# Masked softmax of an attention stage: exponent and mask read the scaled scores from the PSUM score banks, or from a float32 copy in SBUF

## Chip, cores and metric

The kernel runs on one core of a Trainium2 chip. The metric is the device time of one execution in microseconds (us), lower is better. In the profile PE is TensorE (matmuls), PEld its weight loads, DVE is VectorE, ACT is ScalarE, POOL is GpSimd and SP is SyncE. PSUM is the memory that TensorE writes its results to (8 banks of 512 float32 per partition); SBUF is the larger on-chip memory. TensorE writes to PSUM only, and GpSimd does not read PSUM in this program.

## What is computed

Three stages follow each other. The change lies in the first, the attention, with q, k and v of shape (4, 8, 576, 64), so 32 heads:

```python
scale = 1.0 / np.sqrt(q.shape[-1])
scores = scale * np.matmul(q, k.transpose(0, 1, 3, 2))
thresh = np.max(scores, axis=-1, keepdims=True) - tau
scores = np.where(scores >= thresh, scores, -1000000000.0)
scores = scores - np.max(scores, axis=-1, keepdims=True)
attn = np.exp(scores)
attn = attn / (np.sum(attn, axis=-1, keepdims=True) + 1e-09)
return np.matmul(attn, v).astype(np.float32)
```

Its output (2304 tokens of 512) goes through a gated layer, `(x @ w_a) * (x @ w_b) @ w_out`, and then through a second layer with a softmax-like activation and a layer norm. Everything is float32; the two later stages split each operand into a high and a low part and use three matmuls for each product.

## The kernel before

**Work of the attention stage.** Two heads make a pair; there are NP = 16 pairs. A pair has NS = 9 units of 128 score rows (two heads times four blocks of 128 queries, and one unit that holds the last 64 queries of both heads), each 576 keys wide, which makes 144 units. The loop over `m` takes two units a step, called A and B here, so 72 steps work on new scores and nine steps make two pairs.

**What a unit passes through.** `scores` (line 277) multiplies q and k into one of two PSUM buffers `ps`, each of two banks. `soft_max` (line 283, DVE) reads the scores, multiplies them by -SCALE, takes the row minimum of the products into `nm`, and writes the products to a bfloat16 tile `junk` that nobody reads and of which there is one buffer. `soft_exp` (line 295, ACT) reads the scores from `ps` again and writes exp(SCALE * score + nm) to `pe` (`pet` for the unit of the last queries). `soft_thr` (line 300, POOL) turns `nm` into the threshold `th`, a column of 128 numbers. `soft_mask` (line 309, DVE) reads the scores from `ps` a third time, compares them with `th`, multiplies `pe` by the comparison in place, and sums each row into `z`. Below, these four are called max, exp, threshold and mask. One step later the masked unit is transposed on TensorE (`tpose`, line 329, into `tp`; `tpose_tail`, lines 345 and 348, into `tq`), copied to SBUF by ACT (line 322), and some steps later multiplied with v (`pv`, line 360, into `po`; copied out by ACT at line 368). Line 381 transposes the reciprocals of the row sums.

**What sets the order.** The order is written out by hand and kept by a manual schedule: each engine works through its own instructions in the order in which the program issues them. Within a step it is the string

```python
PROG = 'ABtVFTUYaufbz'
```

`A` and `B` are scores, max and exp of the two units, `t` and `u` the two thresholds, `a` and `b` the two masks; `V` are the products with v, `F` the transposed reciprocals, `T`, `U` and `Y` the transposes of the units of the step before. `f` and `z` are filling work on DVE: the reciprocal of the row sums (lines 315 and 316) or one of three operations (lines 125, 128 and 131) that assemble later stages' weights from pairs of 32-bit words. At the end of a step ACT gets the copies (lines 322, 368) and parts of the same weight conversion (lines 121 and 135), POOL the last part of it (line 138), and SP the loads. So DVE's order in a step is max A, max B, mask A, filling work, mask B, filling work, and TensorE's is scores A, scores B, products with v, transposes.

**Who waits for whom.** The waits are put in from the buffers: scores A of a step take the `ps` buffer of unit A of the step before, and must wait until its last reader is done with it; the same holds for B.

Of the kernel before, what the change touches and what calls it, by code (L numbers as in the profile page):

```python
# [8 lines left out]
F32 = mybir.dt.float32  # L9
F32R = mybir.dt.float32r  # L10
BF16 = mybir.dt.bfloat16
U32 = mybir.dt.uint32
U64 = mybir.dt.uint64
AF = mybir.ActivationFunctionType
ALU = mybir.AluOpType
AX = mybir.AxisListType
PSUM = bass.MemoryType.PSUM
P = 128
# [3 lines left out]
def kernel(  # L22
# [11 lines left out]
    nc = tc.nc  # L34
    NP, _, VS, D = v.shape
# [11 lines left out]
    HS = S // 2  # L47
# [9 lines left out]
    SCALE = 1.0 / float(D) ** 0.5  # L57
    BIG = 3.0e38
# [13 lines left out]
    taub = const.tile([P, 1], F32, name="taub")  # L72
    neg = const.tile([P, 1], F32, name="neg")
    toff = const.tile([P, 1], F32, name="toff")
# [144 lines left out]

    def tau_consts():  # L220
        nc.vector.tensor_scalar(out=neg, in0=taub, scalar1=0.0, scalar2=None, op0=ALU.is_lt)
        nc.vector.tensor_scalar(out=taub, in0=taub, scalar1=-1.0 / SCALE, scalar2=None, op0=ALU.mult)
        nc.vector.scalar_tensor_tensor(out=toff, in0=neg, scalar=BIG, in1=taub, op0=ALU.mult, op1=ALU.add)

    def attention():
        es = ExitStack()
# [2 lines left out]
        pp = es.enter_context(tc.tile_pool(name="pp", bufs=3))  # L229
# [5 lines left out]
        st = {}  # L235
# [42 lines left out]
            st[i, s] = ps  # L278

        def soft_max(i, s, nm):  # L280
            ps = st[i, s]
            junk = pp.tile([P, 2, HS], BF16, name="junk", bufs=1)
            nc.vector.tensor_scalar(out=junk, in0=ps[:, :, 0:HS], scalar1=-SCALE, scalar2=None, op0=ALU.mult, op1=ALU.min, accum_out=nm)  # L283
            st[i, s] = (ps, nm)

        def soft_exp(i, s):
            ps, nm = st[i, s]
            if s < 2 * NQ:
                qc, h = divmod(s, 2)
                if h == 0:  # L290
                    st[i, "p", qc] = pp.tile([P, 2, S], F32, name="pe", bufs=4)
                pe = st[i, "p", qc][:, h]
            else:
                pe = pp.tile([P, S], F32, name="pet", bufs=2)
            nc.scalar.activation(out=pe.rearrange("p (g s) -> p g s", g=2), in_=ps[:, :, 0:HS], func=AF.Exp, bias=nm, scale=SCALE)  # L295
            st[i, s] = [ps, pe, nm]

        def soft_thr(nm):
            th = sm.tile([P, 1], F32, name="th")
            nc.gpsimd.tensor_scalar(out=th, in0=nm, scalar1=-1.0 / SCALE, scalar2=toff, op0=ALU.mult, op1=ALU.add)  # L300
            return th

        def soft_mask(i, s, th):
            ps, pe, _ = st[i, s]
            if s == 0:
                st[i, "z"] = sm.tile([P, NS], F32, name="z", bufs=2)
            z = st[i, "z"]
            pv = pe.rearrange("p (g s) -> p g s", g=2)
            nc.vector.scalar_tensor_tensor(out=pv, in0=ps[:, :, 0:HS], scalar=th, in1=pv, op0=ALU.is_ge, op1=ALU.mult, accum_out=z[:, s:s + 1])  # L309
            st[i, s] = pe  # L310

        def recip(i):
# [82 lines left out]
        for h in range(2):  # L395
# [4 lines left out]
            if h == 0:  # L400
                nc.scalar.dma_start(out=taub, in_=tau.to_broadcast([P, 1]))
        tau_consts()
        alloc_qk(1)
        load_k(1)
# [15 lines left out]
        for m in range(tot // 2 + 6):  # L420
# [9 lines left out]
            nm = {}  # L430
            th = {}

            def score(k):
                if k < len(cur):
                    nm[k] = sm.tile([P, 1], F32, name="nm")
                    scores(*cur[k])
                    soft_max(*cur[k], nm[k])
                    soft_exp(*cur[k])

            def thr(k):  # L440
                if k < len(cur):
                    th[k] = soft_thr(nm[k])

            def mask(k):
                if k < len(cur):
                    soft_mask(*cur[k], th[k])
                    if cur[k][1] == NS - 1:
                        recip(cur[k][0])
# [32 lines left out]
            i, s = divmod(2 * m, NS)  # L481
# [312 lines left out]
```

## Time and profile before

| what | us |
|---|---|
| median of three runs (992.99, 994.72, 995.31) | 994.72 |
| the profiled execution: its own time | 994.94 |
| the profiled execution: span from first to last instruction | 993.2 |
| attention stage: first max to the last mask's end | 7.4 to 302.5 |
| PE, DVE, ACT, POOL busy, whole span | 958.6, 552.1, 461.8, 196.1 |

A row of the timeline reads: start in us from the span's start, duration in us, engine, line of the kernel, operation, out<-in by the program's names, and in brackets how long the engine had been idle before and who ended that. Several instructions of one kind in a row are merged (x2, x8), and then the duration is that of all of them. A max or a mask is followed by a short DVE_READ_ACCUMULATOR that writes out its row result. In a group the columns are operation, names, shapes, count | busy us, mean ns of one | idle time before it and its cause. The granted TensorE clock is 0.997 of full speed over the span.

### The profile page before, as it was taken

The page shows a single profiled execution, that of the slowest core. Times are in us where ns is not written, and L with a number is a line of the kernel's source. Part 1 is how long each engine was busy: PE and PEld are TensorE (multiplying, and loading weights), DVE is VectorE, ACT ScalarE, POOL GpSimd, SP SyncE. Part 2 cuts the span into 40 slices and gives each one's busy share as a digit, 9 for nine tenths or more (in the row PEclk, how much of TensorE's full clock was granted, in tenths as well). Part 3 has the DMA queues.
Part 4 walks back from the last instruction along what each step waited for, and adds up shares of the span by engine and source line. Part 5 has one row for each costly group of instructions (what it writes and reads, how often), then busy time and mean ns, then how long its engine had stood idle before and what let it go on. Part 6 is the DMA issues. An engine that isn't in the chain of part 4 may idle for free.

```text
span 993.2 us, 17033 instructions
## 1 busy us (share of the span) xinstructions
PE 958.6 (97%) x6464; PEld 797.9 (80%) x6464; DVE 552.1 (56%) x1262; ACT 461.8 (47%) x889; POOL 196.1 (20%) x294
## 2 busy tenths in 40 slices
PE   6999898999899999999999999999999999999997
PEld 3555555555558999999999999999999788888885
DVE  5888888877887665553222666322322544444443
ACT  4777777777775444443222444211221434333332
POOL 1111112111113311220000333000001233333331
PEclk9999999999999999999999999999999999999999
DMA  5423532432615655444210554222102111111100
GB/s 140 143 85 96 157 103 84 132 96 82 165 59 176 204 169 155 142 134 122 92 49 24 179 156 154 72 73 72 47 26 94 32 50 47 46 49 45 44 22 32
DMA packets 56002, 95.59 MB, mean 96 GB/s; under 512 B 15088, under 2 KB 33648, under 8 KB 55920
## 3 DMA queue, kind: packets, MB, share of 16 engines
q1 hardware_dynamic: 55488, 93.91, 31.0%
q8 instruction: 51, 0.84, 0.4%
q10 hardware_dynamic: 432, 0.59, 0.2%
q14 instruction: 31, 0.25, 0.1%
HBM read 70.80 MB, written 23.68 MB: 95 GB/s over the span
## 4 chain that ended last, share of the span: by engine, by line
PE 83%; DVE 10%; issue 2%; ACT 2%; DMA 1%; POOL 1%; SPq 0%; DVEq 0%; ACTq 0%
PE ps L542 29%; PE py L564 15%; PE po L698 10%; PE ps L646 9%; PE ps L277 7%; PE po L360 7%; PE tp L329 5%; DVE junk L283 3%; DVE pe L309 2%; PE pl L679 1%; DVE pet L309 1%; PE tq L345 1%; DMA wraw<-in_w_dram 1%; DMA k<-in_qkv_dram 1%; DVE w L131 0%
## 5 line engine op out<-in xcount | busy, mean ns | idle before, releaser
L542 PE MATMUL ps<-xt,w 128*128 128x288 f32 x2304 | 321.4, 295 | 0.3 <-DVE g L549 0.2
L542 PEld LDWEIGHTS ps<-xt,w 128*128 128x128 f32 x2304 | 310.9, 188 | 0.7 <-DVE g L549 0.7
L564 PE MATMUL py<-gt,w 128*128 128x288 f32 x1152 | 168.1, 295 | 0.0
L564 PEld LDWEIGHTS py<-gt,w 128*128 128x128 f32 x1152 | 158.0, 188 | 0.0
L549 DVE TENSOR_TENSOR g<-ps,a 128x288 f32<-128x288 f32 x96 | 43.8, 457 | 192.7 <-ACT a L548 192.7
L138 POOL TENSOR_TENSOR w<-w,w 128x512 fp32r<-128x512 f32 x52 | 77.9, 1498 | 289.9 <-ACT w L135 289.9
L283 DVE TENSOR_SCALAR_CACHE_REDUCE junk<-ps 128x576 bf16<-128x576 f32 x144 | 109.0, 757 | 43.2 <-PE ps L277 34.5
L277 PE MATMUL ps<-k,q 64*128 64x288 f32 (+1 forms) x640 | 105.8, 450 | 25.7 <-DVE pe L309 15.8
L548 ACT ACTIVATE a<-ps 128x288 f32<-128x288 f32 x96 | 39.3, 409 | 187.3 <-PE ps L542 187.3
L295 ACT ACTIVATE pe<-ps,nm 128x576 f32<-128x576 f32 x128 | 94.8, 743 | 66.3 <-DVE junk L283 65.3
L698 PE MATMUL po<-w,lt 128*128 128x512 f32 x432 | 104.5, 395 | 2.6 <-ACT lt L684 1.3
L309 DVE SCALAR_TENSOR_TENSOR pe<-ps,th,pe 128x576 f32<-128x576 f32 x128 | 104.0, 816 | 5.0 <-POOL th L300 3.2
L646 PE MATMUL ps<-w,ys 128*128 128x512 f32 x432 | 105.2, 398 | 1.3 <-POOL ys L518 1.3
L698 PEld LDWEIGHTS po<-w,lt 128*128 128x128 f32 x432 | 80.4, 187 | 23.6 <-ACT lt L684 2.2
L277 PEld LDWEIGHTS ps<-k,q 64*128 64x128 f32 (+1 forms) x640 | 47.3, 179 | 62.3 <-issue 26.4
L646 PEld LDWEIGHTS ps<-w,ys 128*128 128x128 f32 x432 | 79.6, 187 | 20.3 <-POOL ys L518 1.7
L322 ACT ACTIVATE pt<-tp 128x512 f32<-128x512 f32 (+1 forms) x160 | 79.0, 552 | 7.7 <-PE tp L329 5.8
L300 POOL TENSOR_SCALAR th<-nm,toff 128x1 f32<-128x1 f32 x144 | 38.1, 265 | 216.3 <-DVE junk L283 214.2
L360 PE MATMUL po<-pt,vr 128*64 128x322 f32 (+1 forms) x512 | 78.3, 427 | 0.1
L329 PEld LDWEIGHTS tp<-ident,pe 128*128 128x128 f32 x512 | 58.0, 145 | 24.8 <-issue 17.4
L329 PE MATMUL tp<-ident,pe 128*128 128x128 f32 x512 | 72.9, 285 | 0.9 <-ACT pt L322 0.9
L551 DVE TENSOR_TENSOR gt<-g,gt 128x288 fp32r<-128x288 f32 x96 | 44.0, 458 | 49.1 <-ACT gt L550 49.1
(73 smaller groups left out, 802.3 us busy)
## 6 DMA issues: line engine op xcount, KB each, us to landing
wraw<-in_w_dram SPq DMA_DIRECT2D x36, 512.0 KB
q<-in_qkv_dram SPq DMA_DIRECT2D x15, 576.0 KB
k<-in_qkv_dram SPq DMA_DIRECT2D x30, 176.0 KB
xd<-xp SPq DMA_DIRECT2D x16, 289.0 KB
xr<-xd SPq DMA_DIRECT2D x8, 576.0 KB
zr<-rzd SPq DMA_DIRECT2D x16, 288.0 KB
xsd<-xr SPq DMA_DIRECT2D x8, 576.0 KB
ypd<-y SPq DMA_DIRECT2D x8, 576.0 KB
```

Source lines behind the costliest of these rows:

```text
L138: nc.gpsimd.tensor_tensor(out=w["o"][1], in0=w["f"] if wide else raw, in1=w["o"][0].bitcast(F32), op=ALU.subtract)
L277: nc.tensor.matmul(ps[rows, g, 0:HS], lhsT=q[r, u, c], rhs=k[r, u, o:o + HS], start=True, stop=True, skip_group_check=True)
L283: nc.vector.tensor_scalar(out=junk, in0=ps[:, :, 0:HS], scalar1=-SCALE, scalar2=None, op0=ALU.mult, op1=ALU.min, accum_out=nm)
L295: nc.scalar.activation(out=pe.rearrange("p (g s) -> p g s", g=2), in_=ps[:, :, 0:HS], func=AF.Exp, bias=nm, scale=SCALE)
L309: nc.vector.scalar_tensor_tensor(out=pv, in0=ps[:, :, 0:HS], scalar=th, in1=pv, op0=ALU.is_ge, op1=ALU.mult, accum_out=z[:, s:s + 1])
L322: evac_q.append(lambda: nc.scalar.activation(out=out, in_=in_, func=AF.Copy))
L329: nc.tensor.transpose(tp[:, kc, :], pe[:, o:o + P], ident)
L360: nc.tensor.matmul(po[h * D:(h + 1) * D], lhsT=lhsT, rhs=rhs, start=(kc == 0), stop=(kc == NQ), skip_group_check=True)
L542: nc.tensor.matmul(pa[:, 0:NB], lhsT=wt[:, m, wi, kc * P:(kc + 1) * P], rhs=xt[:, kc, xi, :], start=(k == 0), stop=(k == 3 * KC - 1))
L564: nc.tensor.matmul(py, lhsT=wt[:, 2, wi, oc * P:(oc + 1) * P], rhs=gt[:, gi, :], start=(first and k == 0), stop=(last and k == 2))
L646: nc.tensor.matmul(ph[:, g, :], lhsT=y[:, a, kc, :], rhs=w2(2 * kc + g, b), start=(k == 0), stop=(k == 3 * KC - 1))
L698: nc.tensor.matmul(po, lhsT=lt[:, a, j, :], rhs=w2(2 * KC + j, b), start=(k == 0), stop=(k == 3 * NJ - 1))
```

## The change

The max now writes its products, -SCALE times the scores, as float32 to a new SBUF tile `ns` with four buffers, in place of the bfloat16 `junk`. The exp reads `ns` with scale -1, and the mask reads `ns` and compares with "less or equal", so that neither touches `ps` any more. The threshold is formed in the scaled domain; one tiny instruction of the preparation goes.

```diff
     def tau_consts():
         nc.vector.tensor_scalar(out=neg, in0=taub, scalar1=0.0, scalar2=None, op0=ALU.is_lt)
-        nc.vector.tensor_scalar(out=taub, in0=taub, scalar1=-1.0 / SCALE, scalar2=None, op0=ALU.mult)
-        nc.vector.scalar_tensor_tensor(out=toff, in0=neg, scalar=BIG, in1=taub, op0=ALU.mult, op1=ALU.add)
+        nc.vector.scalar_tensor_tensor(out=toff, in0=neg, scalar=-BIG, in1=taub, op0=ALU.mult, op1=ALU.add)
...
         def soft_max(i, s, nm):
-            ps = st[i, s]
-            junk = pp.tile([P, 2, HS], BF16, name="junk", bufs=1)
-            nc.vector.tensor_scalar(out=junk, in0=ps[:, :, 0:HS], scalar1=-SCALE, scalar2=None, op0=ALU.mult, op1=ALU.min, accum_out=nm)
-            st[i, s] = (ps, nm)
+            ns = pp.tile([P, 2, HS], F32, name="ns", bufs=4)
+            nc.vector.tensor_scalar(out=ns, in0=st[i, s][:, :, 0:HS], scalar1=-SCALE, scalar2=None, op0=ALU.mult, op1=ALU.min, accum_out=nm)
+            st[i, s] = (ns, nm)
...
-            nc.scalar.activation(out=pe.rearrange("p (g s) -> p g s", g=2), in_=ps[:, :, 0:HS], func=AF.Exp, bias=nm, scale=SCALE)
-            st[i, s] = [ps, pe, nm]
+            nc.scalar.activation(out=pe.rearrange("p (g s) -> p g s", g=2), in_=ns, func=AF.Exp, bias=nm, scale=-1.0)
+            st[i, s] = (ns, pe)
...
-            nc.gpsimd.tensor_scalar(out=th, in0=nm, scalar1=-1.0 / SCALE, scalar2=toff, op0=ALU.mult, op1=ALU.add)
+            nc.gpsimd.tensor_scalar(out=th, in0=nm, scalar1=1.0, scalar2=toff, op0=ALU.mult, op1=ALU.add)
...
-            nc.vector.scalar_tensor_tensor(out=pv, in0=ps[:, :, 0:HS], scalar=th, in1=pv, op0=ALU.is_ge, op1=ALU.mult, accum_out=z[:, s:s + 1])
+            nc.vector.scalar_tensor_tensor(out=pv, in0=ns, scalar=th, in1=pv, op0=ALU.is_le, op1=ALU.mult, accum_out=z[:, s:s + 1])
```

No instruction changes its place on its engine; what differs are the operands, and with them the waits that stand in front of instructions. Lines after the first of these edits move up: in the changed kernel scores are line 276, max 281, exp 293, threshold 298, mask 307, transposes 327.

On DVE, two steps around a weight conversion, first before. The brackets give the engines whose progress the instruction waits for (`DVE_49` is DVE's own, `PE_49` TensorE's).

```order
L283 TENSOR_SCALAR junk,nm<-ps 128x576 [waits DVE_49,PE_49] x2
L309 SCALAR_TENSOR_TENSOR pe,z<-ps,th,pe 128x576 [waits Activation_49,Pool_49]
L125 TENSOR_SCALAR wlow<-wraw 128x512 [waits DMAHW3_49]
L309 SCALAR_TENSOR_TENSOR pe,z<-ps,th,pe 128x576 [waits Activation_49,Pool_49]
L128 SCALAR_TENSOR_TENSOR wlow<-wraw,wlow 128x512 [waits DVE_49]
L283 TENSOR_SCALAR junk,nm<-ps 128x576 [waits PE_49]
L283 TENSOR_SCALAR junk,nm<-ps 128x576 [waits DVE_49,PE_49]
```

The same place in the changed kernel:

```order
L281 TENSOR_SCALAR ns,nm<-ps 128x576 [waits PE_49] x2
L307 SCALAR_TENSOR_TENSOR pe,z<-ns,th,pe 128x576 [waits Activation_49,Pool_49]
L125 TENSOR_SCALAR wlow<-wraw 128x512 [waits DMAHW3_49]
L307 SCALAR_TENSOR_TENSOR pe,z<-ns,th,pe 128x576 [waits Activation_49,Pool_49]
L128 SCALAR_TENSOR_TENSOR wlow<-wraw,wlow 128x512 [waits DVE_49]
L281 TENSOR_SCALAR ns,nm<-ps 128x576 [waits PE_49] x2
```

The order is the same; max B no longer waits for an earlier instruction of DVE (the one buffer of `junk` is gone).

On TensorE, the transposes of one step and the scores of the next, before:

```order
L329 MATMUL tp<-ident,pe 128x128 [waits Activation_49]
L329 MATMUL tp<-ident,pe 128x128 x3
L277 MATMUL ps<-k,q 128x288 [waits DVE_49,PE_49]
L277 MATMUL ps<-k,q 128x288
```

and in the changed kernel:

```order
L327 MATMUL tp<-ident,pe 128x128 [waits DVE_49,Activation_49]
L327 MATMUL tp<-ident,pe 128x128 x3
L276 MATMUL ps<-k,q 128x288 [waits DVE_49]
L276 MATMUL ps<-k,q 128x288
```

Both versions let the scores wait for DVE, but for another instruction: the last reader of `ps` was the mask and is now the max. The transposes now carry a wait for DVE of their own, for the mask whose output they read; before, the scores ahead of them in TensorE's order had waited for that mask already.

## Rows read from the trace of the kernel before

**Rows 1.** Windows: busy us of each engine in nine steps of the attention stage.

```profile
103.19:139.99 36.80, 33.98 (x252) 19.78 (x250) 31.14 (x83) 27.70 (x52) 7.32 (x20) 1.00 0.36 112
```

**Rows 2.** Waits from 5 to 303 us: in total us, times, longest us.

```profile
DVE junk L283 <- PE ps L277: 34.5, 50, 2.4
...
PE ps L277 <- DVE pe L309: 15.8, 20, 1.7
```

**Rows 3.** Timeline: a step without filling work (DVE, ACT and POOL).

```profile
132.05 0.75 DVE L283 TENSOR_SCALAR_CACHE_REDUCE junk<-ps 128x576 bf16<-128x576 f32 x1
...
132.84 0.74 ACT L295 ACTIVATE pet<-ps,nm 128x576 f32<-128x576 f32 x1 [0.92 <-DVE junk L283]
132.93 0.76 DVE L283 TENSOR_SCALAR_CACHE_REDUCE junk<-ps 128x576 bf16<-128x576 f32 x1
...
133.68 0.82 DVE L309 SCALAR_TENSOR_TENSOR pet<-ps,th,pet 128x576 f32<-128x576 f32 x1
133.73 0.74 ACT L295 ACTIVATE pe<-ps,nm 128x576 f32<-128x576 f32 x1 [0.15 <-DVE junk L283]
133.87 0.26 POOL L300 TENSOR_SCALAR th<-nm,toff 128x1 f32<-128x1 f32 x1 [0.63 <-DVE junk L283]
...
134.57 0.82 DVE L309 SCALAR_TENSOR_TENSOR pe<-ps,th,pe 128x576 f32<-128x576 f32 x1
...
135.45 0.76 DVE L283 TENSOR_SCALAR_CACHE_REDUCE junk<-ps 128x576 bf16<-128x576 f32 x1
```

**Rows 4.** Timeline of DVE: mask A, L125, mask B, L128, next max.

```profile
113.31 0.82 DVE L309 SCALAR_TENSOR_TENSOR pe<-ps,th,pe 128x576 f32<-128x576 f32 x1
...
114.39 0.81 DVE L309 SCALAR_TENSOR_TENSOR pet<-ps,th,pet 128x576 f32<-128x576 f32 x1
...
115.73 0.75 DVE L283 TENSOR_SCALAR_CACHE_REDUCE junk<-ps 128x576 bf16<-128x576 f32 x1
```

**Rows 5.** Groups of DVE in the nine steps of rows 1.

```profile
L131 DVE SCALAR_TENSOR_TENSOR w<-w,wlow 128x512 uint32<-128x512 uint32 x2 | 1.4, 688 | 0.0
```

**Rows 6.** Timeline of TensorE over the nine steps.

```profile
102.39 1.24 PE L277 MATMUL ps<-k,q 64*128 64x288 f32 x8
...
105.82 0.76 PE L277 MATMUL ps<-k,q 64*128 64x288 f32 x4
...
107.84 1.31 PE L360 MATMUL po<-pt,vr 128*64 128x322 f32 x8
...
110.86 1.40 PE L277 MATMUL ps<-k,q 64*128 64x288 f32 x12
...
134.65 1.65 PE L277 MATMUL ps<-k,q 64*128 64x288 f32 x8
136.23 1.08 PE L360 MATMUL po<-pt,vr 128*64 128x256 f32 x8
...
139.18 1.24 PE L277 MATMUL ps<-k,q 64*128 64x288 f32 x8
```

**Rows 7.** Groups of the gated layer: the same operation from PSUM and from SBUF.

```profile
L549 DVE TENSOR_TENSOR g<-ps,a 128x288 f32<-128x288 f32 x96 | 43.8, 457 | 192.7 <-ACT a L548 192.7
L548 ACT ACTIVATE a<-ps 128x288 f32<-128x288 f32 x96 | 39.3, 409 | 187.3 <-PE ps L542 187.3
L551 DVE TENSOR_TENSOR gt<-g,gt 128x288 fp32r<-128x288 f32 x96 | 44.0, 458 | 49.1 <-ACT gt L550 49.1
L550 ACT ACTIVATE gt<-g 128x288 fp32r<-128x288 f32 x96 | 42.7, 445 | 54.3 <-DVE g L549 54.3
```

**Rows 8.** Timeline: DVE and POOL operations that read two SBUF tiles, at the same time.

```profile
306.47 0.69 DVE L128 SCALAR_TENSOR_TENSOR wlow<-wraw,wlow 128x512 uint32<-128x512 uint32 x1
...
306.71 1.59 POOL L138 TENSOR_TENSOR w<-w,w 128x512 fp32r<-128x512 f32 x1 [5.46 <-ACT w L135]
...
307.26 1.59 DVE L131 SCALAR_TENSOR_TENSOR w<-w,wlow 128x512 uint32<-128x512 uint32 x1
```

**Rows 9.** Groups of POOL from 5 to 303 us.

```profile
L138 POOL TENSOR_TENSOR w<-w,w 128x512 fp32r<-128x512 f32 x12 | 15.3, 1279 | 29.8 <-ACT w L135 29.8
```

More of the change, by code (lines that the diff above doesn't have):

```diff
@@ L280, in soft_max @@
         def soft_max(i, s, nm):
-            ps = st[i, s]
-            junk = pp.tile([P, 2, HS], BF16, name="junk", bufs=1)
-            nc.vector.tensor_scalar(out=junk, in0=ps[:, :, 0:HS], scalar1=-SCALE, scalar2=None, op0=ALU.mult, op1=ALU.min, accum_out=nm)
-            st[i, s] = (ps, nm)
+            ns = pp.tile([P, 2, HS], F32, name="ns", bufs=4)
+            nc.vector.tensor_scalar(out=ns, in0=st[i, s][:, :, 0:HS], scalar1=-SCALE, scalar2=None, op0=ALU.mult, op1=ALU.min, accum_out=nm)
+            st[i, s] = (ns, nm)
         def soft_exp(i, s):
-            ps, nm = st[i, s]
+            ns, nm = st[i, s]
             if s < 2 * NQ:
@@ L294, in soft_exp @@
                 pe = pp.tile([P, S], F32, name="pet", bufs=2)
-            nc.scalar.activation(out=pe.rearrange("p (g s) -> p g s", g=2), in_=ps[:, :, 0:HS], func=AF.Exp, bias=nm, scale=SCALE)
-            st[i, s] = [ps, pe, nm]
+            nc.scalar.activation(out=pe.rearrange("p (g s) -> p g s", g=2), in_=ns, func=AF.Exp, bias=nm, scale=-1.0)
+            st[i, s] = (ns, pe)
         def soft_thr(nm):
             th = sm.tile([P, 1], F32, name="th")
-            nc.gpsimd.tensor_scalar(out=th, in0=nm, scalar1=-1.0 / SCALE, scalar2=toff, op0=ALU.mult, op1=ALU.add)
+            nc.gpsimd.tensor_scalar(out=th, in0=nm, scalar1=1.0, scalar2=toff, op0=ALU.mult, op1=ALU.add)
             return th
         def soft_mask(i, s, th):
-            ps, pe, _ = st[i, s]
+            ns, pe = st[i, s]
             if s == 0:
```

## The prediction

> **What bounds the kernel now.** I read the attention stage first, since nothing else changes. Of its 72 steps I took nine (two pairs of heads, after which the pattern repeats) and asked with the windows view which engine fills them [rows 1]: 36.80 us, with TensorE busy for 33.98, DVE for 31.14 and ACT for 27.70. None is full, and two are nearly so. The waits view says what lies between these two [rows 2]: the max waits 34.5 us in all for scores, and the scores wait for masks (15.8 us that the view shows; more is hidden below). So the two hold each other up: mask A and B of one step must end before scores A and B of the next may overwrite the bank, and the next max must wait for those scores.
>
> What would each engine need without waiting? For DVE, the timeline of a step without filling work [rows 3] runs max A at 132.05, max B 0.88 later, mask A 1.63, mask B 2.52, next max A 3.40. Filling work pushes this out [rows 4]: with L125 between the masks they stand 1.08 apart and not 0.89 (+0.19); with L128 behind mask B the next max comes 1.34 after it and not 0.88 (+0.46). L131 runs as long as L128 (688 ns) and occurs twice in the nine steps [rows 5]; I give it the same 0.46. L125 and L128 also occur twice each, and the two small operations of the reciprocal add an estimated 0.15 per pair. DVE's need: 9 x 3.40 + 2 x 0.46 + 2 x (0.19 + 0.46) + 2 x 0.15 = 33.1 us.
>
> For TensorE, the nine steps go from 102.39 to 139.18, 36.79 us [rows 6]. Scores of a step that run straight through take 1.24 us, and what follows starts about 0.07 before that end (134.65 + 1.65 against 136.23), so 1.17. At 105.82 it was 2.02 until the products began, 0.85 too long; there are five such places, the last at 134.65 with 0.41, and they sum to 3.9. TensorE's need: 36.79 - 3.9 = 32.9 us. Both needs are about 10% below the 36.80.
>
> **The change, part by part.**
>
> *The score bank comes free at the max.* Scores A and B of the next step can start as soon as TensorE reaches them. It reaches them after the transposes of the step before, and those need only masks that are a whole step older. This removes the 3.9 us per nine steps. What is late next on that path is the transposes, which wait for mask B of the step before; they come about 1.2 us (scores) plus the products later in TensorE's order, and this is the lead that TensorE can build up.
>
> *Max B no longer waits for max A to be written out* (the one buffer of junk). It can follow 0.75 after max A, as a mask follows a max (132.93 to 133.68 [rows 3]). That alone does not bring mask A forward, for mask A then waits for exp A.
>
> *Exp reads SBUF.* In the gated layer ACT's copy of 288 columns takes 409 ns from PSUM and 445 from SBUF [rows 7]: +36 ns. So exp A starts 0.79 after max A (132.84) as now, lasts 0.74 + 0.036, and a mask follows an exp's end by 0.10 (133.73 + 0.74 to 134.57 [rows 3]): mask A at 1.68, against 1.63. On ACT, with 5 us per nine steps to spare at the new pace, it is covered otherwise.
>
> *Mask reads two SBUF tiles.* The multiply from PSUM and SBUF took 457 ns, the one from two SBUF tiles 458 [rows 7]: no difference, and I leave the mask at 0.82. The max writes float32 where it wrote bfloat16; at 576 elements in 0.76 us I take that as free too, the multiplies [rows 7] having float32 outputs and the same time per element (457 ns for 288). The instruction saved in the preparation is 0.15 us at most, once. The Trainium skill, "VectorE: DVE Perf Modes", section on the TRN2 errata, has a smaller fixed cost for VectorE from SBUF than from PSUM (58 against 120 cycles, some 65 ns). By that figure the 144 masks would save an estimated 9 us more; the groups show nothing of it [rows 7], and I go by these.
>
> *Mask and threshold meet at one port.* This is the cost to weigh. A POOL operation on two SBUF tiles starts at 306.71 [rows 8], while DVE works on two SBUF tiles until 307.16, and ends at 308.30: 1.59 us where the same takes 1.28 [rows 9], as if it had begun with 0.13 of its work already behind it at 307.16. L131, issued at 307.26, in turn took 1.59 and not 0.69. They take turns. Until now the mask had one operand in PSUM, and the threshold B that ran beside it took its plain 0.26 [rows 3]. The Trainium skill, "SBUF — State Buffer", section "Who interferes with whom", says so as a rule: a VectorE instruction with two SBUF inputs and a GpSimd instruction that reads SBUF exclude each other for their whole length; the trace agrees [rows 8].
>
> Threshold B starts 0.94 after max B (132.93 to 133.87). With max B at 0.75 that is 1.69, a dead heat with mask A at 1.68. So threshold B will mostly sit out mask A (until 2.50), end 0.13 later and let mask B go at about 2.67 instead of the 2.43 that exp B allows (0.75 + 0.79 + 0.78 + 0.10, rounded). The next max follows 0.73 behind, as in the rows with filling work. The three prices of a step without filling work: 3.16 with no contention, 3.40 with the turn-taking just worked out, 3.53 if the threshold needs its full 0.26 after the mask. Of the nine steps:
>
> - three without filling work: 3.16 / 3.40 / 3.53 each;
> - two with the reciprocal (+0.15): 3.31 / 3.55 / 3.68;
> - two with L131 between the masks, itself with two SBUF inputs, behind which the threshold may have to wait again: 3.76 / 3.89 / 4.14;
> - two with L125 and L128: 4.10 / 4.23 / 4.49.
>
> Sums: 31.8 / 33.5 / 35.2 us. I take the middle one, nearest to what L138 showed [rows 8]. Against 36.80 it saves 3.3 us per nine steps.
>
> *DVE and TensorE must still interlock.* In four of the nine steps TensorE needs more than DVE: at 105.82 to 110.86, less the 0.85, 4.19 us; the last, 134.65 to 139.18 less 0.41, 4.12; all four exceed DVE's new steps by 2.3 together. With TensorE's lead none of that shows; without any lead all of it does, and 1.0 of the 3.3 is left. Following the nine steps by hand, TensorE keeps more than 1 us ahead, so I charge 0.5.
>
> **Sum.** 36.80 - 33.5 - 0.5 = 2.8 us per nine steps, times eight: 22 us. The later stages are only moved forward. Against the profiled execution's 994.94 that is 973 us; that execution stands 0.2 above the median of the three runs, which I ignore. Bounds: without contention TensorE's 32.9 is the floor, 8 x 3.9 = 31 us, giving 964; with the dearest contention 8 x 1.6 = 13, giving 982; with no lead at all 8 x 1.0 = 8, giving 987.
>
> **The rivals.**
>
> *TensorE becomes the bound and has no lead* (987 us). For it: the two needs differ by under 1 us in nine steps, and ACT copies the transposes only after both exps, which may hold the products. Against: the slack found by following the steps. Chance 0.13, with anything from 982 to 990.
>
> *The port decides: slower.* In this stage POOL runs L138 twelve times for 1.28 us each [rows 9], and the thresholds queue behind it. If an L138 waits for a mask and then holds the next mask for its whole length with a threshold behind, that is up to 1.28 + 0.26 = 1.54 us on DVE's path, 18.5 us in twelve. Together with the dearest turn-taking, which leaves 13, this ends about 6 us slower, 1000 us. It decides from about 1.1 us per L138. For it: L131's 1.59 [rows 8]. Against: L138 follows ACT's L135, which comes after the masks of its step, and meets mostly maxes, which read PSUM. Chance 0.08. The rule of the Trainium skill named above would act here too; it does not say how often the two meet.
>
> *The release does nothing.* If something other than the mask held scores and products all along, such as ACT's copies of the transposes, the new waits end when the old ones did: 993 to 997 us. For it: ACT's copies stand behind the exps in its order. Against: [rows 2] name the mask. Chance 0.06.
>
> **Chances.** Forecast (964 to 982) 0.73; the other cases as above. About 0.2%, 2 us, is what a measurement of this kernel can tell from no change. Faster by more than that: 0.73 + 0.13 = 0.86; same 0.06; slower 0.08. The range is 963 to 986 us, from the floor by TensorE to most of the first rival.
>
> **What would show it.** Right: no wait of scores for a mask; max B 0.75 behind max A; mask A about 1.68 after max A; some thresholds stretched from 0.26 to nearly 1 us; nine steps in about 34 us; the last mask ending near 280. Exp near 0.78 and mask near 0.82. Wrong: nine steps still above 36; masks well above 0.82 us; TensorE waiting more than 1 us per step in front of the transposes, or thresholds that start late behind L138 with DVE idle beside them.

## The result

The changed kernel takes 965.79 us (median of four runs, 965.45 to 966.18) against 993.93 for the kernel before (four runs): ratio 0.9716, 95% interval [0.9699, 0.9733], 28 us faster. Predicted were 973 us within 963 to 986.

The groups of the changed kernel that answer to the pieces of the change (columns as before: names, shapes, count | busy us, mean ns of one | idle time before it and its cause):

```profile
L293 ACT ACTIVATE pe<-ns,nm 128x576 f32<-128x576 f32 x128 | 94.0, 775 | 47.4 <-DVE ns L281 47.2
L307 DVE SCALAR_TENSOR_TENSOR pe<-ns,th,pe 128x576 f32<-128x576 f32 x128 | 102.7, 815 | 16.0 <-ACT pe L293 12.7
...
L281 DVE TENSOR_SCALAR_CACHE_REDUCE ns<-ps 128x576 f32<-128x576 f32 x144 | 102.7, 750 | 9.8 <-PE ps L276 9.3
...
L276 PE MATMUL ps<-k,q 64*128 64x288 f32 (+1 forms) x640 | 96.0, 439 | 4.4 <-DMA k<-in_qkv_dram 4.2
...
L298 POOL TENSOR_SCALAR th<-nm,toff 128x1 f32<-128x1 f32 x144 | 38.4, 269 | 186.7 <-DVE ns L281 186.7
```

The wait for the mask is gone from TensorE's score matmuls: of the 4.4 us that they idle, 4.2 are a load at the start; before, 15.8 were the mask [rows 2]. The max waits 9.3 us for scores in place of 34.5 [rows 2]. The mask kept its time (815 ns), the exp went to 775, the mean threshold hardly moved (269).

Nine steps, in the windows view, from one TensorE score block to the one nine steps later, over the same pattern as the nine steps of [rows 1] (us: length, then busy PE, PEld, DVE, ACT, POOL, granted clock, DMA share, GB/s):

```profile
98.41:131.70 33.29, 32.76 (x251) 19.96 (x250) 30.33 (x83) 26.44 (x52) 6.02 (x19) 1.00 0.41 126
```

33.29 us where it was 36.80, 3.5 us saved; times eight that is 28 us. The stretches differ a little: seven in a row take 32.92 in the mean (33.20 to 263.62), and three in a row of the kernel before, at the same granted clock of 1.00, took 36.29 (38.32 to 147.20), which is 3.4 saved. Either way the nine steps account for the gain, to about a microsecond. TensorE is now busy for 32.76 of the 33.29, and the 0.53 left are one wait, for ACT:

```profile
106.08 0.44 PE L343 MATMUL tq<-ident,pe 128*128 128x128 f32 x2 [0.53 <-ACT zt L384]
```

Line 384 is ACT's copy of the transposed reciprocals out of PSUM. ACT has it behind both exps of the step, and the transposes of line 343 use the same set of buffers.

One step as it begins (timeline, DVE, ACT and POOL), with L125 as its first filling work:

```profile
99.21 0.76 DVE L281 TENSOR_SCALAR_CACHE_REDUCE ns<-ps 128x576 f32<-128x576 f32 x1
...
99.90 0.75 DVE L281 TENSOR_SCALAR_CACHE_REDUCE ns<-ps 128x576 f32<-128x576 f32 x1
100.02 0.77 ACT L293 ACTIVATE pe<-ns,nm 128x576 f32<-128x576 f32 x1 [0.35 <-DVE ns L281]
...
100.83 0.27 POOL L298 TENSOR_SCALAR th<-nm,toff 128x1 f32<-128x1 f32 x1 [0.41 <-DVE ns L281]
100.89 0.82 DVE L307 SCALAR_TENSOR_TENSOR pe<-ns,th,pe 128x576 f32<-128x576 f32 x1 [0.23 <-ACT pe L293]
```

Max B follows max A by 0.69, threshold B starts 1.62 after max A and mask A 1.68. The dead heat went to the threshold, by 0.06 us. It is 0.27 us long and mask A 0.82, so neither is stretched, though they overlap for 0.21.

DVE alone in a step without filling work:

```profile
125.18 0.69 DVE L281 TENSOR_SCALAR_CACHE_REDUCE ns<-ps 128x576 f32<-128x576 f32 x1
...
126.79 0.82 DVE L307 SCALAR_TENSOR_TENSOR pe<-ns,th,pe 128x576 f32<-128x576 f32 x1 [0.23 <-ACT pe L293]
...
127.53 0.82 DVE L307 SCALAR_TENSOR_TENSOR pe<-ns,th,pe 128x576 f32<-128x576 f32 x1
...
128.31 0.76 DVE L281 TENSOR_SCALAR_CACHE_REDUCE ns<-ps 128x576 f32<-128x576 f32 x1
```

3.13 us from max to max, where it was 3.40 [rows 3]; mask B stands 0.74 behind mask A. This max A follows the reciprocal and is short; over the 29 such steps from 10 to 265 us in which DVE does not wait after mask A, the median is 3.16.

### The profile page after: what moved, and what is told of

Its sections match the earlier page's. It is cut to its first block, busy times and chain, and to the rows that moved or that the text cites. A ratio compares the mean times of both kernels' runs of the same rounds, so it can differ in the third digit from the quotient of the medians.

```text
span 964.4 us, 16891 instructions
## 1 busy us (share of the span) xinstructions
PE 947.0 (98%) x6464; PEld 797.9 (83%) x6464; DVE 541.5 (56%) x1261; ACT 457.2 (47%) x889; POOL 196.2 (20%) x294
## 4 chain that ended last, share of the span: by engine, by line
PE 88%; DVE 5%; DMA 2%; ACT 2%; issue 1%; SPq 1%; POOL 0%; DVEq 0%; ACTq 0%
PE ps L540 30%; PE py L562 15%; PE po L696 10%; PE ps L644 9%; PE ps L276 8%; PE po L358 7%; PE tp L327 6%; PE pl L677 1%; DVE pe L307 1%; DMA wraw<-in_w_dram 1%; DMA k<-in_qkv_dram 1%; PE tq L343 1%; ACT pe L293 1%; DVE ns L281 1%; DVE xr L199 0%
## 5 line engine op out<-in xcount | busy, mean ns | idle before, releaser
L138 POOL TENSOR_TENSOR w<-w,w 128x512 fp32r<-128x512 f32 x52 | 78.0, 1501 | 288.9 <-ACT w L135 288.9
L293 ACT ACTIVATE pe<-ns,nm 128x576 f32<-128x576 f32 x128 | 94.0, 775 | 47.4 <-DVE ns L281 47.2
L307 DVE SCALAR_TENSOR_TENSOR pe<-ns,th,pe 128x576 f32<-128x576 f32 x128 | 102.7, 815 | 16.0 <-ACT pe L293 12.7
L281 DVE TENSOR_SCALAR_CACHE_REDUCE ns<-ps 128x576 f32<-128x576 f32 x144 | 102.7, 750 | 9.8 <-PE ps L276 9.3
L276 PE MATMUL ps<-k,q 64*128 64x288 f32 (+1 forms) x640 | 96.0, 439 | 4.4 <-DMA k<-in_qkv_dram 4.2
```

Of the source, the lines that this page charges most:

```text
L138: nc.gpsimd.tensor_tensor(out=w["o"][1], in0=w["f"] if wide else raw, in1=w["o"][0].bitcast(F32), op=ALU.subtract)
L276: nc.tensor.matmul(ps[rows, g, 0:HS], lhsT=q[r, u, c], rhs=k[r, u, o:o + HS], start=True, stop=True, skip_group_check=True)
L281: nc.vector.tensor_scalar(out=ns, in0=st[i, s][:, :, 0:HS], scalar1=-SCALE, scalar2=None, op0=ALU.mult, op1=ALU.min, accum_out=nm)
L307: nc.vector.scalar_tensor_tensor(out=pv, in0=ns, scalar=th, in1=pv, op0=ALU.is_le, op1=ALU.mult, accum_out=z[:, s:s + 1])
```

## The experiments

Medians in us; the ratio is to the kernel before, timed on the same chip.

| run | median | ratio, 95% interval |
|---|---|---|
| changed kernel | 965.79 | 0.9716 [0.9699, 0.9733] |
| e1_junk4 | 992.85 | 0.9986 [0.9970, 1.0002] |
| e2_mask_bank | 994.28 | 1.0004 [0.9991, 1.0018] |
| e3_exp_bank | 969.39 | 0.9758 [0.9743, 0.9773] |
| e4_thr_two_ops | 976.92 | 0.9833 [0.9818, 0.9847] |
| e11_before_thr_two | 996.49 | 1.0034 [1.0021, 1.0047] |
| e5_pe_more | 977.13 | 0.9822 [0.9791, 0.9853] |
| e6_dve_more | 970.75 | 0.9759 [0.9735, 0.9784] |
| e9_ns2 | 964.15 | 0.9693 [0.9669, 0.9716] |
| e7_later_x | 964.53 | 0.9694 [0.9667, 0.9721] |
| after_b | 965.01 | 0.9713 [0.9701, 0.9726] |
| e9b_ns2 | 964.45 | 0.9709 [0.9697, 0.9722] |
| e10_ns2_later_x | 964.07 | 0.9705 [0.9693, 0.9718] |

### Which part of the change pays?

**e1_junk4**, one part alone:

```diff
-            junk = pp.tile([P, 2, HS], BF16, name="junk", bufs=1)
+            junk = pp.tile([P, 2, HS], BF16, name="junk", bufs=4)
```

> The kernel before with four buffers of junk instead of one and nothing else: max B no longer waits for max A to be written out, but the score bank is still held until the mask. Theory (the gain comes from the bank that comes free at the max): most of the gain is missing, 984 to 994 us. Rival (the gain comes from max B's wait on DVE itself): 966 to 972 us.

Measured 992.85, within the range of the theory, the interval reaching 1. From its waits view, 5 to 300 us (us in total, times, longest):

```profile
DVE junk L283 <- PE ps L277: 33.2, 61, 2.1
...
PE ps L277 <- DVE pe L309: 16.5, 22, 1.7
```

Max B came earlier (0.69 behind max A in the median, where it was 0.89), and the score bank was held until the mask as before: the waits of [rows 2] are all still there. While the bank is held, max B's own wait is worth at most 0.3%, some 3 us, and cannot be told from nothing.

**e2_mask_bank**, the exp from the copy and the mask from the bank (kernel before, edited):

```diff
-            junk = pp.tile([P, 2, HS], BF16, name="junk", bufs=1)
-            nc.vector.tensor_scalar(out=junk, in0=ps[:, :, 0:HS], scalar1=-SCALE, scalar2=None, op0=ALU.mult, op1=ALU.min, accum_out=nm)
+            ns = pp.tile([P, 2, HS], F32, name="ns", bufs=4)
+            nc.vector.tensor_scalar(out=ns, in0=ps[:, :, 0:HS], scalar1=-SCALE, scalar2=None, op0=ALU.mult, op1=ALU.min, accum_out=nm)
...
-            nc.scalar.activation(out=pe.rearrange("p (g s) -> p g s", g=2), in_=ps[:, :, 0:HS], func=AF.Exp, bias=nm, scale=SCALE)
+            nc.scalar.activation(out=pe.rearrange("p (g s) -> p g s", g=2), in_=ns, func=AF.Exp, bias=nm, scale=-1.0)
```

> The max writes the float32 copy, the exp reads the copy, the mask reads the score bank as before, so the bank is held until the mask. Theory (bank): 986 to 998 us, scores wait for the mask as before. Rival (max B's own wait, or anything about the copy itself): 966 to 975 us.

Measured 994.28, no gain. Everything of the change is in but the mask's read (and with it the threshold, which stays in the unscaled domain), and all of the gain is gone; the scores wait for the mask as before:

```profile
PE ps L277 <- DVE pe L309: 17.1, 22, 1.7
```

**e3_exp_bank**, the other way round (changed kernel, edited):

```diff
...
-            nc.scalar.activation(out=pe.rearrange("p (g s) -> p g s", g=2), in_=ns, func=AF.Exp, bias=nm, scale=-1.0)
+            nc.scalar.activation(out=pe.rearrange("p (g s) -> p g s", g=2), in_=ps[:, :, 0:HS], func=AF.Exp, bias=nm, scale=SCALE)
```

> The changed kernel, but the exp reads the score bank; the mask reads the copy. The bank comes free at the end of the exp, some 1.5 (A) and 2.3 us (B) after max A. Theory (TensorE now sets the pace and reaches the next scores about 2.6 us after max A): no difference from the changed kernel, 964 to 968 us; the exp is 0.035 us shorter, which buys nothing. Rival (the moment of release matters down to the max): 972 to 985 us.

Measured 969.39, between the two ranges: 24 of the 28 us are there, 3.6 are missing. The waits view, 5 to 300 us, names the exp:

```profile
PEld ps L276 <- ACT pe L293: 13.3, 36, 1.2
DVE ns L281 <- PE ps L276: 13.3, 25, 2.3
```

The first row counts weight loads (PEld), and these sit idle between blocks in the changed kernel too, so it is no measure of lost time. What TensorE loses shows in its matmuls: the scores behind one block of transposes, in this run and then at the same place of the changed kernel:

```profile
110.41 1.09 PE L327 MATMUL tp<-ident,pe 128*128 128x128 f32 x8
111.64 1.44 PE L276 MATMUL ps<-k,q 64*128 64x288 f32 x8
```

```profile
107.89 1.09 PE L327 MATMUL tp<-ident,pe 128*128 128x128 f32 x8
108.91 1.24 PE L276 MATMUL ps<-k,q 64*128 64x288 f32 x8
```

The scores start 1.23 after the transposes and not 1.02, and take 0.20 longer. In the changed kernel TensorE had reached them here 1.39 after max A (107.52 to 108.91), not the 2.6 of the expectation. Over seven stretches of nine steps (34.57 to 268.38) the mean is 33.40 us against 32.92; times eight that is 3.9, about the missing 3.6. Releasing the bank at the exp gives most of the gain, at the max the rest. So it is the bank, and it is the mask that held it.

### The port of mask and threshold

**e4_thr_two_ops**, the threshold in two POOL operations, in the changed kernel:

```diff
-            nc.gpsimd.tensor_scalar(out=th, in0=nm, scalar1=1.0, scalar2=toff, op0=ALU.mult, op1=ALU.add)
+            t0 = sm.tile([P, 1], F32, name="t0")
+            nc.gpsimd.tensor_scalar(out=t0, in0=nm, scalar1=1.0, scalar2=toff, op0=ALU.mult, op1=ALU.add)
+            nc.gpsimd.tensor_scalar(out=th, in0=t0, scalar1=1.0, scalar2=zoff, op0=ALU.mult, op1=ALU.add)
```

(`zoff` is a column of zeros.)

> The changed kernel with the threshold formed in two POOL operations, so that the second one of unit B comes while mask A runs. Port theory (the changed kernel is spared the contention only because threshold B starts 0.06 us ahead of mask A): the second operation is stretched to 0.6 to 0.8 us, mask B starts about 1.0 us after mask A in place of 0.75, DVE's need in nine steps rises by about 2 us over TensorE's: 971 to 979 us. Rival (so small an operation does not meet the mask at the port): second operation at 0.26 us, 965 to 968 us.

Measured 976.92, 11 us above the changed kernel. One step of its timeline (masks are line 309 here, the second threshold operation line 300):

```profile
118.29 0.27 POOL L299 TENSOR_SCALAR t<-nm,toff 128x1 f32<-128x1 f32 x1
118.35 0.82 DVE L309 SCALAR_TENSOR_TENSOR pe<-ns,th,pe 128x576 f32<-128x576 f32 x1 [0.41 <-POOL th L300]
118.65 0.65 POOL L300 TENSOR_SCALAR th<-t,zoff 128x1 f32<-128x1 f32 x1
...
119.34 0.82 DVE L309 SCALAR_TENSOR_TENSOR pe<-ns,th,pe 128x576 f32<-128x576 f32 x1 [0.16 <-POOL th L300]
```

The second operation starts under mask A, takes 0.65 in place of 0.27 and ends 0.13 after mask A; mask B follows 0.04 later, 0.99 after mask A. These are the numbers that the prediction had charged to the changed kernel itself. The first operation starts 0.06 ahead of mask A and keeps its 0.27. Of the 144 second operations 71 take 0.65 us or more.

**e11_before_thr_two**, the same edit in the kernel before, where the mask has one operand in PSUM:

> The kernel before with the threshold formed in two POOL operations: the mask still reads the score bank and one SBUF tile. Port theory: the second operation of unit B runs beside mask A at its plain 0.26 us; if it ends later than exp B, mask B waits for the difference of under 0.1 us a step, 993 to 999 us. Rival (a POOL operation beside a mask is stretched wherever the mask reads, or two operations are simply too long a path): stretched to 0.6 us or more, 1003 to 1006 us, 11 us more as in the changed kernel.

Measured 996.49, 3 us above the kernel before; by the waits view DVE's masks wait 7.5 us for thresholds in place of 4.4, which is about that. The second operation over all 144 units (duration in ns: least, median, most), and one that runs under a mask:

```profile
L302 POOL TENSOR_SCALAR th<-t,zoff x144: 264/264/268, 8.1 to 301.0; 128x1 f32<-128x1 f32 x144
```

```profile
131.12 0.82 DVE L311 SCALAR_TENSOR_TENSOR pe<-ps,th,pe 128x576 f32<-128x576 f32 x1
131.24 0.26 POOL L301 TENSOR_SCALAR t<-nm,toff 128x1 f32<-128x1 f32 x1 [0.26 <-DVE junk L283]
131.60 0.27 POOL L302 TENSOR_SCALAR th<-t,zoff 128x1 f32<-128x1 f32 x1
```

Never stretched. So it is the mask with two SBUF operands that shuts POOL out; with one operand in PSUM it does not. The rule of the Trainium skill, "SBUF — State Buffer", section "Who interferes with whom", says that a VectorE instruction contends with a GpSimd one that reads SBUF if it has two SBUF inputs, and not if it has at most one (outside the modes in which it reads through both ports). The traces agree on both halves: 0.65 us and more against 0.27 in e4, 264 to 268 ns in e11. They do not show a threshold holding a mask up: one that starts 0.06 ahead of it costs the mask nothing (0.82).

### What sets the pace now?

**e5_pe_more**, one transpose of each unit twice (the changed kernel):

```diff
-            for kc in range(NQ):
+            for kc in [0] + list(range(NQ)):
                 o = kc * P + (D if s < 2 * NQ and s % 2 else 0)
```

> The changed kernel with the first of the four transposes of each unit done twice: about 0.13 us more on TensorE per unit, 144 units, 18 us, and nothing more on the other engines. Theory (TensorE sets the pace of the attention stage now): most of it shows, 980 to 985 us. Rival (DVE sets the pace, TensorE waits for it): 966 to 971 us.

Measured 977.13: 11.3 us more than the changed kernel, between the ranges. The transposes of one step, in the run and then in the changed kernel, each with what follows:

```profile
101.68 1.31 PE L327 MATMUL tp<-ident,pe 128*128 128x128 f32 x10
102.83 0.38 PE L343 MATMUL tq<-ident,pe 128*128 128x128 f32 x2
```

```profile
97.17 1.09 PE L327 MATMUL tp<-ident,pe 128*128 128x128 f32 x8
98.10 0.38 PE L343 MATMUL tq<-ident,pe 128*128 128x128 f32 x2
```

1.15 against 0.93: the edit costs TensorE 0.22 in this step, 16 us in 72 steps, of which 11.3, or 70%, show in the time. The windows view has seven stretches of nine steps, from score block to score block, again in the run and then in the changed kernel:

```profile
34.14:276.21 242.07, 241.96 (x1878) 153.38 (x1877) 208.13 (x567) 191.35 (x360) 47.34 (x137) 1.00 0.40 116
```

```profile
33.20:263.62 230.42, 228.90 (x1751) 139.53 (x1750) 207.13 (x569) 187.10 (x360) 47.05 (x137) 1.00 0.41 122
```

TensorE's busy time grows by 13.1 us in these 63 steps and the stretch by 11.7, so of what is added to TensorE 89% shows in the stage; the rest went into the 1.5 us that TensorE had idle in the changed kernel and that are 0.1 here. TensorE sets the pace. In 72 steps 11.7 become 13.3; that the time shows 2 us less stays open. The expectation's price, 0.13 a unit, was too high: 13.1 us in 126 units are 0.10.

**e6_dve_more**, a write of zeros on DVE between the masks of a step:

```diff
...
+                    if ch == "b" and cur:
+                        nc.vector.memset(pad, 0.0)
                     mask("ab".index(ch))
```

> The changed kernel with a write of 240 zeros per partition to an unused tile on DVE between mask A and mask B of each step: about 0.25 us more on DVE per step, 72 steps, 18 us. Theory (TensorE sets the pace, and DVE has some 0.15 us a step to spare): about half of it shows, 971 to 977 us. Rival (DVE sets the pace): nearly all of it, 981 to 985 us.

Measured 970.75, 5.0 us more. A step of it:

```profile
99.33 0.82 DVE L307 SCALAR_TENSOR_TENSOR pe<-ns,th,pe 128x576 f32<-128x576 f32 x1 [0.24 <-ACT pe L293]
...
100.15 0.26 DVE L472 MEMSET pad<- 128x240 f32 x1
100.33 0.70 DVE L307 SCALAR_TENSOR_TENSOR pe<-ns,th,pe 128x576 f32<-128x576 f32 x1
...
100.95 0.75 DVE L281 TENSOR_SCALAR_CACHE_REDUCE ns<-ps 128x576 f32<-128x576 f32 x1
```

The masks stand 1.00 apart instead of 0.74, but the next max follows mask B after 0.62 and not after some 0.74: the edit costs DVE about 0.14 a step, 10 us, and not the 18 that the expectation was written with. Half of that shows (and the time lies just under the range of the theory, which had the higher price). It reaches TensorE by the one wait that its matmuls have left (waits view, 20 to 265 us, in the changed kernel and then in e6_dve_more):

```profile
PE tq L343 <- ACT zt L384: 1.4, 3, 0.5
```

```profile
PE tq L343 <- ACT zt L384: 4.1, 6, 1.1
```

So TensorE sets the pace and passes on most of an added cost; DVE has little to spare and passes on about half. With TensorE slowed, the max waits for scores again (waits view, 20 to 265 us, e5_pe_more and then the changed kernel):

```profile
DVE ns L281 <- PE ps L276: 15.8, 27, 1.2
```

```profile
DVE ns L281 <- PE ps L276: 6.3, 10, 0.8
```

### What else

**e9_ns2** and **e9b_ns2**, `bufs=2` for the copy instead of 4:

> The changed kernel with two buffers of the float32 copy instead of four. The next step's max must then wait for the mask of the same half of the step before, an instruction that DVE has started before it anyway, and must let it end first. Theory: the wait costs DVE up to 0.15 us a step, less than it has to spare: 965 to 969 us. Rival (the copies must reach over two steps): 972 to 985 us.

> The changed kernel again, as the reference for the two runs beside it: 964 to 967 us.

> The changed kernel with two buffers of the copy, again, beside the changed kernel on one chip. Theory (two buffers are enough and change nothing): within 1 us of the run beside it. Rival (the 1.6 us between them in the earlier runs is real): 1 to 2 us faster.

Measured 964.15, just under the range of the theory, and beside the changed kernel on one chip 964.45 against 965.01, intervals overlapping: no difference that can be told, and the 1.6 us of the first comparison did not come back. Max B stood 0.69 behind max A in the trace, so the wait of a max for a mask of the step before costs nothing; two buffers are enough.

**e7_later_x** and **e10_ns2_later_x**, the start of the gated layer:

```diff
-            prep = n < n1 and f in (2, 3)
+            prep = n < n1 and f in (3, 4)
...
-                if n == 0:
+                if n == 1:
                     load_x(1)
...
-                        prep_x(j + 1, f - 2)
+                        prep_x(j + 1, f - 3)
...
-                    prep_x2(0, 2 * f - 4)
+                    prep_x2(0, 2 * f - 6)
```

(e10 has `bufs=2` as well.)

> The changed kernel; in the gated layer the load of the second block of tokens is issued one unit later, behind the weight load, and its preparation one unit later too. Theory (2 us of the gain are given back at the start of the gated layer, where a weight load lands late behind that load): 963.5 to 965 us. Rival (that wait only moves): 965.5 to 968 us.

> Two buffers of the copy, and the load and preparation of the second block of tokens one unit later. Theory (the start of the gated layer gives back some 2 us of the gain): 1.5 to 2 us faster than the changed kernel beside it. Rival: no difference.

The reason to try it is in the changed kernel's timeline:

```profile
293.04 0.43 DVE L125 TENSOR_SCALAR wlow<-wraw 128x512 uint32<-128x512 uint32 x1 [3.98 <-DMA wraw<-in_w_dram]
...
297.47 3.44 PE L540 MATMUL ps<-xt,w 128*128 128x288 f32 x24 [1.31 <-DVE g L547]
```

A weight load lands late, DVE waits for it, and TensorE waits for DVE. From the first matmul of that layer to the first of its seventh unit it takes 28.3 us (274.74 to 303.03), against 26.3 in the kernel before (307.00 to 333.34). With the edit this wait is gone: in e7 the same stretch takes 26.0 us (275.00 to 301.00), in e10 26.0 (275.69 to 301.64). The times are 964.53, and 964.07 beside 965.01, 0.9 us where 1.5 to 2 were expected: in the direction expected, but within what the runs scatter, so as a faster version it stays open.

## Why the prediction was right, point by point

- **The score bank comes free at the max: right, and it is the gain.** The wait of the score matmuls for the mask went from 15.8 us to none, and e2 shows that without it nothing is gained.
- **Max B without its own wait: right in sign.** Predicted 0.75 behind max A, measured 0.69; worth at most some 3 us alone (e1). Its side effect mattered more, below.
- **Exp from SBUF, mask from two SBUF tiles: right.** Predicted 0.776 and 0.82, measured 0.775 and 0.815; mask A at 1.68 predicted and measured. The smaller fixed cost of SBUF operands on VectorE that the Trainium skill states ("VectorE: DVE Perf Modes", section on the TRN2 errata) did not show: the mask's mean went from 816 ns to 815. That the max would write float32 for free came true (757 to 750 ns), but not for the reason given: 457 ns for 288 elements are 1.59 ns each, the max takes 1.3.
- **Mask and threshold meet at one port: the mechanism right, the term mis-sized.** This is the step that failed. I called threshold B at 1.69 and mask A at 1.68 a dead heat and gave it to the mask. Max B came 0.06 earlier than I had it, so threshold B starts at 1.62, ahead of mask A, and neither is longer for it. I charged 0.24 us a step without filling work (3.40 in place of 3.16); the median is 3.16. The price itself was right: e4 pays it as worked out, 0.99 from mask A to mask B, and is 11 us slower for it. In the changed kernel it was paid once, in the first step, where threshold B started 0.19 behind mask A and took 0.76 (9.37 to 10.13). The rows could not tell the order, so that it fell on the cheap side was luck, and the range held because it reached down to the bound without contention: 965.79 is 2 us from that bound (964) and 7 from the forecast.
- **The sum.** DVE's need was thus the no-contention column: 31.8 us per nine steps forecast, 32.1 from the medians of the steps in which DVE does not wait after mask A (3.16, 3.36 with the reciprocal, 3.76 with L131, 4.18 with L125 and L128). L131 was right at 0.60 there and too dear at 0.46 in the need before: with it a step of the kernel before takes 3.73. TensorE's need, 32.9 forecast, became the floor, and the stage runs on it: 32.92 in the mean of seven stretches, 32.70 of them busy. The interlock of DVE and TensorE, charged 0.5, left only the wait for ACT shown with the result, 0.2 in the mean. Savings of 3.4 to 3.5 per nine steps in place of 2.8 make 5 to 6 of the 7 us between 973 and the result. The last mask ended at 270.2, not near 280; of the 32 us to the 302.5 before, some 3 are dips of the granted clock in that one execution (below).
- **The later stages only move forward: wrong by about 1 to 2 us.** The gated layer's first units lost them to a late weight load (28.3 against 26.3 us above; 27.4 in after_b, 274.85 to 302.25).
- **The rivals.** TensorE became the bound, as the first said, but almost without idling; what it named for itself, ACT's copies behind both exps, is the one wait that is left. The slower one needs L138 to block masks; the whole stage had one threshold above 0.35 us, that of the first step, and no mask above 0.82. Its sign is there, masks that wait for late thresholds, 4.4 us in 12 cases, but it was 4.4 in 11 in the kernel before. That the release does nothing fell with the result.

## What to carry to other kernels

A buffer that one engine fills and others read is held by its last reader: if the first reader passes the data on anyway, let it write a copy that the later ones read, and the producer may write again once the first reader is done. Before pricing the copy, check what the later readers now share: two SBUF operands on VectorE shut GpSimd out. That cost nothing here with the threshold 0.06 us ahead of the mask, and 11 us with an operation that started behind it (e4), so look at what starts just before and just after. When two engines each need about 90% of a stage, removing their mutual wait is worth at most the distance to the larger need.

## What the runs showed that was not expected

- **The spacing on DVE depends on what stands in front.** Behind the plain write of zeros a mask takes 0.70 us and the next max comes 0.62 later (e6); behind a mask it takes 0.82 and the max comes 0.74 later (changed kernel). A max behind the reciprocal is short in the same way (0.69, at 125.18 above). An added DVE operation of 0.26 us thus cost 0.14. Why was not tried.
- **A threshold can be shut out across two DVE operations.** In e4, where L125 follows mask A, the second threshold operation took 0.99 us, from 121.98 to 122.97, through the mask and the L125 that ended at 122.92. With L131 there it took 1.26, the longest of the run.
- **Short dips of the granted clock at no fixed place.** The changed kernel's profiled execution shows 0.86 over ten microseconds near its end (a mean over the stretch; full speed is 2.4 GHz, the lower level 1.2), with TensorE busy and at 1.00 in the ten before, and the kernel before shows 0.96 over twice 40 us in the attention stage; after_b shows 1.000 throughout, and its span is 962.1. The rows, of the changed kernel and of the one before:

```profile
930.00:940.00 10.00, 10.00 (x53) 8.25 (x53) 3.81 (x9) 3.52 (x6) 3.27 (x4) 1.00 0.08 28
940.00:950.00 10.00, 8.08 (x29) 5.85 (x28) 3.96 (x10) 3.60 (x7) 3.25 (x4) 0.86 0.07 26
```

```profile
180.00:220.00 40.00, 37.26 (x262) 21.75 (x264) 32.66 (x86) 28.66 (x54) 7.63 (x22) 0.96 0.35 105
220.00:260.00 40.00, 37.47 (x268) 22.08 (x266) 32.63 (x86) 29.44 (x56) 7.53 (x21) 0.96 0.46 129
```

What makes it fall there was not tried. It is worth some 1 to 3 us of a single profile (an estimate: 0.14 of 10 us, and 0.04 of 80), and one reason to take the gain from the nine steps and the medians rather than from the two spans.
